# The first table of token numbers from the lists' columns by numbers in GpSimd's registers, and the last batch's ranks later

## The chip, the cores and the metric

The kernel runs on one core of one Trainium2 chip. The metric is the device time of one execution in microseconds (us). TensorE is called PE here, VectorE DVE, ScalarE ACT, GpSimd POOL and SyncE SP, as the profile calls them; PEld is PE's loading of weights. A name with a q (ACTq, SPq) is that engine's sequencer.

## The reference

Attention with rotary positions for 8 batches, 8 heads, 576 positions and a head size of 64; its output is 4608 tokens of 512 numbers. Each token then goes to one of 8 experts, the one with the largest logit, and the expert's two matrices are applied to it:

```
q_rot, k_rot = rotate(q), rotate(k)
attn = softmax(q_rot @ k_rot.T / sqrt(64));  x = attn @ v          # 4608 x 512
logits = x @ w_gate;  e_idx = argmax(logits, axis=1)               # 8 experts
gate_w = softmax(logits)[e_idx];  eom = sigmoid(x @ w_output_gate)
for e in range(8):
    mask = e_idx == e
    h = maximum(x[mask] @ w1[e], 0)                                # 512 x 1024
    out[mask] = gate_w[mask] * eom[mask, e] * (h @ w2[e])          # 1024 x 512
```

## The kernel before, in words

**Attention.** Two heads make a pair, four pairs a batch: 32 pairs, numbered 0 to 31. A pair has nine steps, so there are 288 steps g. In a step PE makes the scores of 128 query rows against 576 keys (`scores`, L468 and L461) in one of two PSUM buffers with the tag "sc"; DVE takes the row maxima (`peak`, L474); ACT makes the exponentials and frees the PSUM buffer (`exp`, L483); a step later DVE transposes them in blocks (`turn`, L489). PE's products with the values (`values`, L511) stand between the scores in four pieces per pair. POOL makes the rotated queries and keys of later pairs (`mult` L417, `add` L421, `keylo` and `querylo` L399). `Attention.step` issues the scores, the maximum and the exponential of a step, then whatever is noted for it in `todo` under four places (0 to 3), so the order on every engine is fixed by the step numbers in `EVENTS` and in the list `fs` that `place` returns.

**Ranks and lists.** After the last pair of a batch `place` works out each token's expert and its rank in that expert's list. It is spread over the following steps: `s0` (sums of the logits, L578 to L580), `s2` and `s3` (L588 on POOL, then the exponential L591 on ACT, which stands in ACT's row between two softmax steps), `s14` (ranks by two matmuls, L661 and L662, then L666 on DVE), `s17` (row and column numbers, L678 to L683), `ones` (five times: the one-hot rows `ro`, L691 on DVE, and `pl`, L693 on POOL), `s20` (the matmul L701) and `s21` (L704), which adds the batch to `lists`, a 128 x 288 table in SBUF. Column j of `lists` holds 128 places of a list; each expert owns 36 columns. For the last batch `place` returns a plain list of pieces, which the second phase takes in its order.

**The first table.** The second phase works in slots: five of 256 tokens from the batches 0 to 5 (their table is called 0), nine more of 256 and up to fifteen of 128 tokens from all of them. `table0` makes table 0 during the last attention steps, from step 266 on: PE transposes `lists` into PSUM (`turned`, L825, in a "sc" buffer), ACT copies it out and sends it to DRAM (L829 to L833), DVE works out which ten columns are wanted (`sums`, `taken`, `slots`; L762 to L799), POOL fetches those ten rows by an indirect DMA (L801), DVE decodes them (L808 to L811), PE transposes them back (L816, again a "sc" buffer) and DVE writes the numbers `0idx` (L817). At step 284 POOL gathers the tokens of the first two slots from DRAM, four indirect DMAs of 128 rows (`fetch`, `gather`, L950).

**Second phase.** For a slot PE transposes the tokens (L980), ACT and DVE split them into a high and a low half (`turn`, L995 and L996), and PE runs through eight pieces j: four products with w1 (`first`, L1015, 2.85 us each) and four with w2 (`second`, L1057, twelve matmuls each). Weights come through SP (L963) and are split by ACT (L972) and DVE (L974); in slot 0 the piece 5 is split on POOL (the condition `2 < u < 8` and `j % 4 == 1`). Results go out by indirect DMAs on POOL (L1069). After each j the method `slot` takes two pieces (one after the first two) of the list `left`: first the last batch's pieces, then those of `table1`. SP reads an expert's number into its registers by `value_load` (L961) before it loads a slot's weights.

Of the kernel before, what the change touches and what calls it, by code (L numbers as in the profile page):

```python
# [13 lines left out]
I32 = mybir.dt.int32  # L14
# [6 lines left out]
NP = H // 2  # L21
# [96 lines left out]
def body(ctx, tc, nb, offs, qk, v, rope, cst, gates, w, out):  # L118
# [115 lines left out]
class Attention:  # L234


    def __init__(self, tc, nb, pools, cc, ident, ii, first, trib, oneb, cnt, zero, qk, v, xd, row, lists):
        nc = tc.nc
        px, px2, pa2, pp1, pp2, ps_s, small, ps_a = pools
        NT = nb * S  # L240
        own = []
        self.inits = []

        def init(bd, z, rz, ac):
            nc.gpsimd.memset(ac[:, NCH - 1, :, :], 0.0)
# [12 lines left out]
        for n in range(npair):  # L258
            self.pairs.append(Pair(tc, pools, n, own[n % 2], ident, ii, rt, qk[n // NP, n % NP], v[n // NP, n % NP]))
        self.pairs[0].raw = raw0  # L260

        self.todo = {}
        self.last = []
        at = self.at
        xbs = {}

        def newxb(b):
            xbs[b] = px2.tile([P, NCH, RW], F32, tag="xb", name=f"xb{b}")

            nc.gpsimd.memset(xbs[b][QR:P, NCH - 1, DM:], 0.0)  # L270

        for n, pr in enumerate(self.pairs):
            g, b = 9 * n, n // NP
            fs = {"kh": lambda pr=pr: pr.keyhi("A"), "kl": lambda pr=pr: pr.keylo("P"),
                  "qh": lambda pr=pr: pr.queryhi("A"), "ql": lambda pr=pr: pr.querylo("P"), "lasts": pr.lasts, "den0": pr.den0, "den1": pr.den1, "den2": pr.den2, "evict": pr.evict, "back": pr.back,
                  "newxb": lambda pr=pr, b=b: newxb(b) if pr.hp == 0 else None}
            fs["divide"] = lambda pr=pr, b=b: pr.divide(xbs[b])
            for t in range(2):
                fs[f"mult{t}"] = lambda pr=pr, t=t: pr.mult("P", t)
                fs[f"add{t}"] = lambda pr=pr, t=t: pr.add("P", t)  # L280
                fs[f"load{t}"] = lambda pr=pr, t=t: pr.load(t)
                fs[f"loadv{t}"] = lambda pr=pr, t=t: pr.loadv(t)
            for k, (b0, b1) in enumerate(PIECES):
                fs[f"av{k}"] = lambda pr=pr, b0=b0, b1=b1: [pr.values(j) for j in range(b0, b1)]
            for name, o, k in EVENTS:
                if n > 1 or name not in ("load1", "load0", "mult1", "add1", "kh", "kl", "mult0", "add0", "qh", "ql")[:10 if n == 0 else 2]:
                    at(g + (3 if name == "lasts" and n == 0 else o), k, fs[name])
            if n % NP == NP - 1:
                fs = place(tc, (px, px2, small), self.pairs, b, NT, cc, trib, oneb, cnt, xbs, xd, row, lists)
                if b == nb - 1:  # L290
                    self.last = fs
                else:
                    self.nplace = 1 + max(k for k, _, _ in fs)
                    for k, p, f in fs:
                        at(g + PLACE + k, p, f)

    def done(self, b):

        return 9 * (NP * b + NP - 1) + PLACE + self.nplace

    def at(self, g, k, f):
        self.todo.setdefault((g, k), []).append(f)
# [252 lines left out]
def place(tc, pools, pairs, b, NT, cc, trib, oneb, cnt, xbs, xd, row, lists):  # L555
# [129 lines left out]
    def ones(c):  # L685

        if c == 0:
            new("ro", [P, NCH, lists.shape[1]], F32R, bufs=1)
            new("pl", [P, NCH, P], F32R, bufs=1)
            new("no", [P, NCH])  # L690
        nc.vector.tensor_scalar(T["ro"][:, c, :], row, T["hr"][:, c:c + 1], 0.0, op0=ALU.is_equal, op1=ALU.add,  # L691
                                accum_out=T["no"][:, c:c + 1])
        nc.gpsimd.tensor_scalar(T["pl"][:, c, :], row[:, 0:P], T["lo"][:, c:c + 1], T["tok"][:, c:c + 1], op0=ALU.is_equal,  # L693
                                op1=ALU.mult)

    def s20():
# [35 lines left out]
class Moe:  # L732
# [115 lines left out]
        V.tensor_tensor(out=out, in0=out, in1=num, op=ALU.min)  # L848

    def table0(self):  # L850
        V, t = self.nc.vector, self.t
        yield from self.turned(0)
        fn, fi = self.padded("fn"), t([P, E], "fi", I32)
        self.t0 = t([P, E], "t0")
        V.tensor_copy(fi, self.cnt)
        V.tensor_scalar(fi, fi, 8, None, op0=ALU.logical_shift_right)
        V.tensor_copy(fn[:, 4:], fi)
        yield
        end = self.sums(fn, "fs")
        yield  # L860
        dl = t([P, E], "fd")
        V.tensor_scalar(dl, fn[:, 4:], -2.0, float(self.rows), op0=ALU.mult, op1=ALU.add)
# [102 lines left out]
    def split(self, u):  # L965
# [215 lines left out]
```

## Time and profile before

| | |
|---|---|
| median of 3 runs | 1076.01 us (1075.89 to 1077.77) |
| the profiled execution | 1075.41 us |
| its span | 1073.6 us, mean granted PE clock 0.985 |
| attention, last softmax activation | at 556.0 us |
| PE busy | 1015.0 us, 95% of the span |
| DVE, ACT, POOL busy | 830.5, 628.0, 606.5 us |

Times inside the execution count from the span's start. A row of the timeline gives the start, the duration of the whole merged group, engine, line, operation, what is written and read, and in brackets the idle time before and what ended it. In a stretch's row "x" counts instructions; PEclk is the granted share of 2.4 GHz, so 0.50 is 1.2 GHz.

### The profile page before, as it was taken

The page shows a single profiled execution, that of the slowest core. Times are in us where ns is not written, and L with a number is a line of the kernel's source. Part 1 is how long each engine was busy: PE and PEld are TensorE (multiplying, and loading weights), DVE is VectorE, ACT ScalarE, POOL GpSimd, SP SyncE. Part 2 cuts the span into 40 slices and gives each one's busy share as a digit, 9 for nine tenths or more (in the row PEclk, how much of TensorE's full clock was granted, in tenths as well). Part 3 has the DMA queues.
Part 4 walks back from the last instruction along what each step waited for, and adds up shares of the span by engine and source line. Part 5 has one row for each costly group of instructions (what it writes and reads, how often), then busy time and mean ns, then how long its engine had stood idle before and what let it go on. Part 6 is the DMA issues. An engine that isn't in the chain of part 4 may idle for free.

```text
span 1073.6 us, 34812 instructions
## 1 busy us (share of the span) xinstructions
PE 1015.0 (95%) x14465; PEld 881.3 (82%) x14465; DVE 830.5 (77%) x1389; ACT 628.0 (58%) x1281; POOL 606.5 (56%) x594
## 2 busy tenths in 40 slices
PE   3999999999999999998989899999999999999995
PEld 3788878878788788887868788899889898899984
DVE  6888898898988888887866866657866867767772
ACT  3466665656666566665544445446765866857762
POOL 4667888788888889788332312214543533542621
PEclk9999999999999999999889999999999999999998
DMA  5556466465555666464347867766977977887860
GB/s 184 158 138 179 144 165 178 142 179 168 161 165 158 161 175 192 124 186 131 78 151 270 274 205 229 233 211 199 346 249 251 333 248 266 315 300 264 282 246 28
DMA packets 58561, 216.48 MB, mean 202 GB/s; under 512 B 9405, under 2 KB 10012, under 8 KB 54304
## 3 DMA queue, kind: packets, MB, share of 16 engines
q1 hardware_dynamic: 50304, 194.03, 57.9%
q0 software_dynamic: 6496, 18.92, 4.9%
q8 instruction: 115, 1.88, 0.7%
q10 hardware_dynamic: 1600, 1.26, 0.4%
q14 instruction: 46, 0.38, 0.1%
HBM read 196.04 MB, written 20.24 MB: 201 GB/s over the span
## 4 chain that ended last, share of the span: by engine, by line
PE 62%; DVE 12%; issue 8%; ACT 7%; POOL 6%; DMA 3%; POOLq 0%; ACTq 0%; SPq 0%; DVEq 0%
PE py L1057 17%; PE ph L1015 13%; PE sc L468 12%; PE acc L511 11%; DVE m L474 4%; PE ph L1007 4%; ACT pm L483 4%; POOL raw L417 3%; DVE pt L489 3%; PE acc L529 1%; PE mtp L980 1%; DMA v<-in_v 1%; DVE xb L536 1%; ACT wh L972 1%; ACT kh L391 1%
## 5 line engine op out<-in xcount | busy, mean ns | idle before, releaser
L483 ACT ACTIVATE pm<-sc,m 128x576 f32<-128x576 f32 x288 | 213.3, 741 | 223.4 <-DVE m L474 222.2
L974 DVE TENSOR_TENSOR wl<-wr,wh 128x1024 fp32r<-128x1024 f32 x183 | 253.4, 1397 | 48.3 <-ACT wh L972 46.8
L474 DVE TENSOR_REDUCE m<-sc 128x1 f32<-128x576 f32 x288 | 212.8, 739 | 77.8 <-PE sc L468 70.2
L468 PE MATMUL sc<-kh,q 64*128 64x288 f32 x1024 | 227.3, 329 | 29.0 <-ACT pm L483 16.3
L489 DVE STREAM_TRANSPOSE pt<-pm 128x576 f32<-128x576 f32 x288 | 219.3, 761 | 0.3 <-ACT pm L483 0.3
L1057 PE MATMUL py<-wh,ht 128*128 128x512 f32 x640 | 216.8, 403 | 0.0
L972 ACT CAST wh<-wr 128x1024 fp32r<-128x1024 f32 x208 | 212.7, 1050 | 0.4 <-ACT lt L832 0.4
L468 PEld LDWEIGHTS sc<-kh,q 64*128 64x128 f32 x1024 | 150.0, 193 | 73.3 <-ACT pm L483 39.4
L511 PE MATMUL acc<-pt,v 32*64 32x160 f32 (+1 forms) x9216 | 202.1, 299 | 4.8 <-PE sc L468 1.9
L511 PEld LDWEIGHTS acc<-pt,v 32*64 32x64 f32 x9216 | 161.3, 133 | 30.0 <-issue 23.3
L417 POOL TENSOR_TENSOR raw<-raw,rt 128x1152 f32<-128x1152 f32 x62 | 164.2, 2648 | 7.9 <-DMA raw<-in_qk 7.7
L1015 PE MATMUL ph<-xt,wh 128*128 128x256 f32 x896 | 161.8, 283 | 0.0
L1057 PEld LDWEIGHTS py<-wh,ht 128*128 128x128 f32 x640 | 121.0, 189 | 25.4
L1015 PEld LDWEIGHTS ph<-xt,wh 128*128 128x128 f32 x896 | 139.5, 190 | 1.8 <-DVE xt L996 0.4
L1015 PE MATMUL ph<-xt,wl 128*128 128x256 f32 x448 | 126.5, 282 | 0.0
L1057 PE MATMUL py<-wl,ht 128*128 128x512 f32 x320 | 126.4, 395 | 0.0
L974 POOL TENSOR_TENSOR wl<-wr,wh 128x1024 fp32r<-128x1024 f32 x25 | 61.0, 2441 | 108.5 <-ACT wh L972 102.0
L468 PE MATMUL sc<-kl,q 64*128 64x288 f32 x512 | 111.9, 300 | 0.0
L421 POOL TENSOR_TENSOR raw<-raw 128x576 f32<-128x576 f32 x62 | 88.2, 1422 | 2.4
L1031 ACT ACTIVATE ht<-ph 128x512 fp32r<-128x512 f32 x56 | 33.4, 597 | 91.1 <-PE ph L1015 91.1
L468 PEld LDWEIGHTS sc<-kl,q 64*128 64x128 f32 x512 | 85.5, 195 | 0.0
L1015 PEld LDWEIGHTS ph<-xt,wl 128*128 128x128 f32 x448 | 85.3, 190 | 0.2 <-DVE wl L974 0.2
(246 smaller groups left out, 1316.7 us busy)
## 6 DMA issues: line engine op xcount, KB each, us to landing
wr<-in_w SPq DMA_DIRECT2D x208, 512.0 KB, 5.1
raw<-in_qk SPq DMA_DIRECT2D x64, 576.0 KB, 4.0
v<-in_v SPq DMA_DIRECT2D x128, 288.0 KB, 5.0
xd<-xb SPq DMA_DIRECT2D x16, 513.0 KB, 7.3
xd<-xb SPq DMA_DIRECT2D x8, 128.2 KB, 5.0
rt<-in_rope ACTq DMA_DIRECT2D x1, 576.0 KB, 5.5
xg<-xd,2idx POOLq DMA_INDIRECT x18, 6.4
out<-y,2idx POOLq DMA_INDIRECT x18, 4.2
```

The source lines that it names most:

```text
L417: self.eng(eng).tensor_tensor(out=rv, in0=rv, in1=self.rt[:, 2 * t:2 * t + 2, x], op=ALU.mult)
L421: self.eng(eng).tensor_tensor(out=r[:, 2 * t, x], in0=r[:, 2 * t, x], in1=r[:, 2 * t + 1, x], op=ALU.add)
L468: nc.tensor.matmul(ps[:, a, :HS], self.q[r, w, c * P:c * P + P], mov[r, a * HS:a * HS + HS], start=(n == 0), stop=(n == 2))
L474: nc.vector.tensor_reduce(self.m[i], ps[:, :, :HS], axis=AX.XY, op=ALU.max, negate=True)
L483: nc.scalar.activation(pe.rearrange("p (a b) -> p a b", a=2), self.ps[i][:, :, :HS], AF.Exp, bias=self.m[i], scale=1.0, accum_out=self.z[: ...
L489: self.nc.vector.transpose(out=self.pt[:, st[0] + 5 * st[1] if st else 4, :], in_=self.pc.pop(i))
L511: nc.tensor.matmul(self.acc[h * D:h * D + D, a, o:o + 32 * n], self.v[r, h, j, :], self.pt[r, u:u + n, 32 * j:32 * j + 32], start=(j == 0) ...
L972: self.nc.scalar.copy(wh, r)
L974: eng.tensor_tensor(out=wl, in0=r, in1=wh.bitcast(F32), op=ALU.subtract)
L1007: nc.tensor.matmul(ph[:, 0, :], st[:, dc, 0:P], mv[:, dc, :], start=(n == 0), stop=(n == 11))
L1015: nc.tensor.matmul(ph[:, f, :], st[:, dc, fs], mv[:, dc, :], start=(n == 0), stop=(n == 11))
L1057: self.nc.tensor.matmul(py[h], st[:, f, hs], mv, start=(f == 0 and n == 0), stop=(f == 7 and n == 2))
```

## The change

`table0` is written anew. Six of its steps run on POOL: the number of full slots per expert (`full`, three operations on a 128 x 8 tile), their running sums (`ends`, three), the column for each slot (`passed`, three; `rows`, four), then `take`: five times a number is read into a POOL register and two columns of `lists` are copied by it, and the decoding (`flags` and `decode`, six operations on 128 x 10 tiles). DVE keeps two small reductions (`counted`), at step 259. Neither the two transposes through PSUM nor the trip through DRAM is left in table 0. Its steps are dated 255 to 269, and the gathers of the first two slots 276, where it was 284. What `table1` needs of the old table's sums (`taken`) is computed in `table1`.

For the last batch three more empty pieces stand ahead of `s14`, and `pl` (L693) is made on DVE; for other batches `V` is POOL, as before. The split of piece 5 in slot 0 goes from POOL to DVE. All later pieces of `left` come three places later.

```diff
-        g = att.done(nb - 3) + 1
-        for k, f in enumerate(pieces(moe.table0(), 19)):
-            att.at(g + k, 2 if k < 18 else 0, f)
-        att.at(g + 18, 2, moe.fetch)
+        g = att.listed(nb - 3)                       # step 262
+        for k, f in moe.table0():
+            att.at(g + k, 2, f)
+        att.at(g + 14, 2, moe.fetch)
...
-        nc.gpsimd.tensor_scalar(T["pl"][:, c, :], row[:, 0:P], ...
+        V.tensor_scalar(T["pl"][:, c, :], row[:, 0:P], ...
...
-                run(s10, s11, s12), run(s13, base), no, s14, no, s14b, run(s15, s16, s17)] + [
+                run(s10, s11, s12), run(s13, base), no, no, no, no, s14, no, s14b, run(s15, s16, s17)] + [
...
+        def full():
+            G.tensor_scalar(fn, self.cnt, 1.0 / SLOT, 0.5 / SLOT - 0.5, op0=ALU.mult, op1=ALU.add)
+            G.tensor_scalar(fn, fn, WHOLE, None, op0=ALU.add)
+            G.tensor_scalar(fn, fn, -WHOLE, None, op0=ALU.add)
+        def ends():
+            a = T["fn"]
+            for k in (1, 2, 4):
+                b = T[f"fs{k}"]
+                G.tensor_tensor(out=b[:, 4:], in0=a[:, 4:], in1=a[:, 4 - k:4 + E - k], op=ALU.add)
+                a = b
+        def passed():
+            G.tensor_scalar(T["fd"], fn, -2.0, float(self.rows), op0=ALU.mult, op1=ALU.add)
+            G.tensor_scalar(T["ge"], end, half, None, op0=ALU.is_le)
+            G.tensor_tensor(out=T["t1"], in0=T["ge"], in1=T["fd"], op=ALU.mult)
+        def counted():
+            V.tensor_reduce(T["ve"], T["ge"], axis=AX.X, op=ALU.add)
+            V.tensor_reduce(T["row"], T["t1"], axis=AX.X, op=ALU.add)
+        def rows():
+            G.tensor_tensor(out=T["row"], in0=T["row"], in1=p, op=ALU.add)
+            G.tensor_copy(ri, T["row"])
+            G.tensor_scalar(T["ve"], T["ve"], float(E - 1), None, op0=ALU.min)
+            G.tensor_copy(ei, T["ve"])
+        def take():
+            for i in range(n0):
+                r = G.value_load(ri[2 * i:2 * i + 1, 0:1], min_val=0, max_val=E * self.rows - 2)
+                G.tensor_copy(tk[:, 2 * i:2 * i + 2], self.lists[:, bass.ds(r, 2)])
...
+        return [(-7, full), (-6, ends), (-5, passed), (-3, counted), (-1, rows), (2, take), (6, flags), (7, decode)]
...
-        eng = self.nc.gpsimd if (self.todo[s][0] == 1 or 2 < u < 8) and j % 4 == 1 else self.nc.vector
+        eng = self.nc.gpsimd if self.todo[s][0] == 1 and j % 4 == 1 else self.nc.vector
```

Three places show what this moves. Line numbers of the kernel after the change differ from those before; the operands tell what is meant. The first place is POOL in pair 28; `kl` and `q` are the low halves for pair 29, `raw` after them is the rotation for pair 30. Before:

```order
L399 TENSOR_TENSOR kl_8655<-raw_8297,kh_8654 128x576
L693 TENSOR_SCALAR pl_8639<-row,lo_8539,tok_8545 128x128 x2
L399 TENSOR_TENSOR q_8729<-raw_8297,q_8729 128x576
L417 TENSOR_TENSOR raw_8609<-raw_8609,rt 128x1152
L693 TENSOR_SCALAR pl_8639<-row,lo_8539,tok_8545 128x128
L421 TENSOR_TENSOR raw_8609<-raw_8609 128x576
```

After, from the operation behind the three of `full`:

```order
L693 TENSOR_SCALAR pl_8657<-row,lo_8557,tok_8563 128x128
L874 TENSOR_TENSOR fs_118<-fn 128x8
L874 TENSOR_TENSOR fs_120<-fs_118 128x8
L874 TENSOR_TENSOR 0fs_122<-fs_120 128x8
L693 TENSOR_SCALAR pl_8657<-row,lo_8557,tok_8563 128x128
L399 TENSOR_TENSOR q_8750<-raw_8315,q_8750 128x576
L417 TENSOR_TENSOR raw_8627<-raw_8627,rt 128x1152
L878 TENSOR_SCALAR 0fd<-fn 128x8
L879 TENSOR_SCALAR 0ge<-0fs_122,ct 128x8
L880 TENSOR_TENSOR 0t_125<-0ge,0fd 128x8
L693 TENSOR_SCALAR pl_8657<-row,lo_8557,tok_8563 128x128
L421 TENSOR_TENSOR raw_8627<-raw_8627 128x576
```

Nine small operations now stand among POOL's large ones, the last three behind the product L417. On DVE two reductions of their results stand in the row of the maxima; after the change, in pair 28 (`m_7` and `m_8` are the maxima of its steps 7 and 8):

```order
L474 TENSOR_REDUCE m_7_8841<-sc_7_8834 128x1
L489 STREAM_TRANSPOSE pt_8615<-pm_6_8830 128x576
L883 TENSOR_REDUCE 0ve<-0ge 128x1
L884 TENSOR_REDUCE 0row<-0t_125 128x1
L474 TENSOR_REDUCE m_8_8890<-sc_8_8883 128x1
```

The maximum of the pair's last step is queued behind them. The second place is POOL in pairs 30 and 31, around the gathers `xg`. Before:

```order
L626 TENSOR_TENSOR ohs_9448<-ohs_9448,ohb_9388 128x8 x2
L801 DMA 0tk<-lst_84,0ri 10x128
L649 TENSOR_TENSOR base_9569<-cnt,ct 128x8
L492 TENSOR_SCALAR rz_110<-z_109 128x10
L629 TENSOR_SCALAR eg_9628<-eg_9628 128x5
L632 TENSOR_TENSOR eg_9628<-eg_9628,sm_9279 128x5
L670 TENSOR_TENSOR pr_9606<-pr_9606,oh_9310 128x40
L950 DMA xg<-xd,0idx 128x513 x4
```

After:

```order
L626 TENSOR_TENSOR ohs_9495<-ohs_9495,ohb_9437 128x8 x4
L994 DMA xg<-xd,0idx 128x513 x4
L649 TENSOR_TENSOR base_9622<-cnt,ct 128x8
L492 TENSOR_SCALAR rz_110<-z_109 128x10
L629 TENSOR_SCALAR eg_9681<-eg_9681 128x5
```

The four gathers are issued ahead of `base`, which DVE's L666 reads, and the fetch of ten rows is gone. The third place is PE in the second phase, where the last batch's ranks (`pl`) are made. Before, between two pieces of `second` of slot 0:

```order
L1057 MATMUL py_1_10347<-wl_10231,ht_0_10127 128x512
L1057 MATMUL py_1_10347<-wh_10230,ht_0_10128 128x512
L661 LDWEIGHTS oneb
L661 MATMUL pl_2_10438<-ohs_10343,oneb 128x48
L662 LDWEIGHTS trib
L662 MATMUL pl_2_10438<-ohb_10337,trib 128x40
L1057 MATMUL py_0_10346<-wh_10247,ht_0_10127 128x512
```

After, behind the first piece of `first` of slot 1:

```order
L1059 MATMUL ph_0_10498<-xt_1_10398,wh_10315 128x256
L1059 MATMUL ph_0_10498<-xt_1_10397,wl_10316 128x256
L661 LDWEIGHTS oneb
L661 MATMUL pl_2_10540<-ohs_10374,oneb 128x48
L662 LDWEIGHTS trib
L662 MATMUL pl_2_10540<-ohb_10368,trib 128x40
L1059 MATMUL ph_1_10543<-xt_1_10397,wh_10361 128x256
```

The ranks stand two pieces of PE's work later: the last of `second` and one of `first`.

## Rows read from the trace of the kernel before

**Rows 1.** Stretches: us, engines' busy time (x), PEclk, DMA share, GB/s.

```profile
428.90:445.40 16.50, 15.92 (x360) 13.45 (x359) 14.10 (x26) 10.11 (x28) 13.36 (x14) 1.00 0.54 151
494.00:517.50 23.50, 21.11 (x363) 17.47 (x362) 16.69 (x35) 10.75 (x30) 16.51 (x17) 0.78 0.27 64
428.90:474.80 45.90, 44.64 (x1044) 37.70 (x1049) 40.40 (x77) 28.53 (x75) 37.34 (x44) 1.00 0.53 148
494.00:556.00 62.00, 56.90 (x1048) 45.81 (x1052) 44.80 (x103) 28.24 (x76) 29.66 (x48) 0.83 0.40 110
506.20:516.40 10.20, 9.63 (x149) 8.20 (x150) 5.66 (x14) 3.71 (x12) 7.28 (x9) 0.50 0.11 30
543.70:553.90 10.20, 10.18 (x132) 6.71 (x121) 3.03 (x7) 1.68 (x5) 4.91 (x8) 0.50 0.44 131
594.90:598.30 3.40, 3.40 (x10) 2.61 (x9) 3.30 (x9) 0.46 (x1) 0.00 (x0) 0.50 0.80 235
```

**Rows 2.** Timeline of PE, around the old table's two transposes.

```profile
506.77 0.85 PE L468 MATMUL sc<-kh,q 64*128 64x288 f32 x2 [1.77 <-ACT pm L483]
...
542.88 0.22 PE L816 MATMUL 0tr<-ident,0tk 10*128 10x10 f32 x1 [1.23 <-ACT pm L483]
543.04 6.36 PE L511 MATMUL acc<-pt,v 32*64 32x160 f32 x80
...
551.72 2.39 PE L511 MATMUL acc<-pt,v 32*64 32x160 f32 x64
```

**Rows 3.** Timeline of POOL in pair 28.

```profile
484.19 1.57 POOL L693 TENSOR_SCALAR pl<-row,lo,tok 128x128 fp32r<-128x128 bf16 x2
486.32 1.42 POOL L399 TENSOR_TENSOR q<-raw,q 128x576 fp32r<-128x576 f32 x1 [0.57 <-ACT q L391]
487.68 2.66 POOL L417 TENSOR_TENSOR raw<-raw,rt 128x1152 f32<-128x1152 f32 x1
```

**Rows 4.** Groups on POOL, 60 to 500 us: busy us, mean ns, idle before.

```profile
L399 POOL TENSOR_TENSOR q<-raw,q 128x576 fp32r<-128x576 f32 x27 | 38.3, 1420 | 25.1 <-ACT q L391 25.1
L399 POOL TENSOR_TENSOR kl<-raw,kh 128x576 fp32r<-128x576 f32 x27 | 38.1, 1409 | 28.4 <-ACT kh L391 28.4
...
L679 POOL TENSOR_SCALAR hr<-hr 128x5 f32<-128x5 f32 x6 | 1.4, 236 | 0.5
```

**Rows 5.** Timeline of DVE in pair 28, the maximum of its last step.

```profile
490.86 0.76 DVE L474 TENSOR_REDUCE m<-sc 128x1 f32<-128x576 f32 x1 [0.54 <-PE sc L468]
```

**Rows 6.** Timeline of POOL, then of ACT, in pair 25.

```profile
441.79 0.27 POOL L588 TENSOR_TENSOR dd<-lgs,mx 128x40 f32<-128x40 f32 x1
...
442.30 0.23 ACT L591 ACTIVATE ex<-dd 128x40 f32<-128x40 f32 x1
```

**Rows 7.** Line 961, SP's register loads: least, median, most ns.

```profile
L961 SPq TENSOR_LOAD <-1ei x12: 268/273/1017, 706.3 to 1020.3; - x12
```

**Rows 8.** Timeline of POOL: first and last of the four gathers.

```profile
543.60 1.12 POOL L950 DMA_INDIRECT xg<-xd,0idx  x1 [3.47 <-DVE 0idx L817]
...
547.66 1.00 POOL L950 DMA_INDIRECT xg<-xd,0idx  x1 [0.30 <-issue]
```

**Rows 9.** Waits of PE, 500 to 660 us: total us, times, longest.

```profile
PE pl L661 <- DVE ohs L626: 2.8, 1, 2.8
PE pl L701 <- POOL pl L693: 2.1, 2, 1.7
```

**Rows 10.** Timeline of PE at the last batch's ranks.

```profile
594.41 0.20 PE L661 MATMUL pl<-ohs,oneb 128*128 128x48 bf16 x1 [2.75 <-DVE ohs L626]
...
598.89 0.40 PE L1015 MATMUL ph<-xt,wh 128*128 128x256 f32 x2
```

**Rows 11.** Timeline of DVE in slot 0.

```profile
581.09 2.86 DVE L974 TENSOR_TENSOR wl<-wr,wh 128x1024 fp32r<-128x1024 f32 x1 [0.49 <-ACT wh L972]
...
595.41 0.68 DVE L996 TENSOR_TENSOR xt<-mtp,xt 128x512 fp32r<-128x512 f32 x1
```

**Rows 12.** The page, part 5: the splits L974 on DVE.

```profile
L974 DVE TENSOR_TENSOR wl<-wr,wh 128x1024 fp32r<-128x1024 f32 x183 | 253.4, 1397 | 48.3 <-ACT wh L972 46.8
```

More of the change, by code (lines that the diff above doesn't have):

```diff
@@ L53 @@
 PLACE, PM = 20, 3
+LISTED = 35
 TURN = 1
@@ L292, in __init__, with listed @@
                 else:
-                    self.nplace = 1 + max(k for k, _, _ in fs)
                     for k, p, f in fs:
                         at(g + PLACE + k, p, f)
-    def done(self, b):
-        return 9 * (NP * b + NP - 1) + PLACE + self.nplace
+    def listed(self, b):
+        return 9 * (NP * b + NP - 1) + PLACE + LISTED
     def at(self, g, k, f):
@@ L692, in ones @@
                                 accum_out=T["no"][:, c:c + 1])
-        nc.gpsimd.tensor_scalar(T["pl"][:, c, :], row[:, 0:P], T["lo"][:, c:c + 1], T["tok"][:, c:c + 1], op0=ALU.is_equal,
+        V.tensor_scalar(T["pl"][:, c, :], row[:, 0:P], T["lo"][:, c:c + 1], T["tok"][:, c:c + 1], op0=ALU.is_equal,
                                 op1=ALU.mult)
@@ L721, in place @@
           (12, 2, adds(1, 2)), (13, 2, adds(3, 4)), (15, 2, s8), (15, 2, base), (17, 1, s14), (17, 2, s14b), (18, 2, s9),
-          (19, 2, lambda: (s10(), s11())), (20, 2, s15), (22, 2, lambda: (s16(), s12())), (23, 2, s17), (35, 1, s20), (35, 2, s21)]
+          (19, 2, lambda: (s10(), s11())), (20, 2, s15), (22, 2, lambda: (s16(), s12())), (23, 2, s17), (LISTED, 1, s20), (LISTED, 2, s21)]
     fs += [(26 + c, 3, lambda c=c: ones(c)) for c in range(NCH)]
@@ L850, in table0 @@
     def table0(self):
[L851 to L862, printed above, removed]
@@ L863, in table0 @@
-        self.taken(self.t0, fn[:, 4:], end, self.n0)
-        yield
-        yield from self.slots(0, 2 * self.n0, end, dl, None, 2, 5, 2)
+        V, G, t = self.nc.vector, self.nc.gpsimd, self.t
+        m, n0 = 2 * self.n0, self.n0
+        sl = self.cc(C_SL)
+        half, p = sl[:, 0:1], sl[:, 1:2]
+        T = {"fn": self.padded("fn"), "fs1": self.padded("fs1"), "fs2": self.padded("fs2")}
+        for n, sh in (("fs4", [P, 4 + E]), ("fd", [P, E]), ("ge", [P, E]), ("t1", [P, E]), ("row", [P, 1]), ("ve", [P, 1])):
+            T[n] = t(sh, f"0{n}")
@@ new lines, in table0 @@
+        fn, end = T["fn"][:, 4:], T["fs4"][:, 4:]
+        self.f0 = fn, end
+        ei, ri = t([P, 1], "0ei", I32), t([P, 1], "0ri", I32)
+        self.ei[0] = ei, 2
+        tk, g1, g2 = (t([P, m], f"0{n}") for n in ("tk", "g1", "g2"))
+        idx = self.idx[0] = t([P, m], "0idx", I32)
+        def full():
+            G.tensor_scalar(fn, self.cnt, 1.0 / SLOT, 0.5 / SLOT - 0.5, op0=ALU.mult, op1=ALU.add)
+            G.tensor_scalar(fn, fn, WHOLE, None, op0=ALU.add)
+            G.tensor_scalar(fn, fn, -WHOLE, None, op0=ALU.add)
@@ new lines, in flags, with decode @@
+        def flags():
+            G.tensor_scalar(g1, tk, 0.0, BIG, op0=ALU.is_equal, op1=ALU.mult)
+            G.tensor_scalar(g2, tk, 0.0, -1.0, op0=ALU.is_gt, op1=ALU.mult)
+            G.tensor_tensor(out=g1, in0=g1, in1=g2, op=ALU.add)
+        def decode():
+            G.tensor_scalar(tk, tk, -number(self.NT, 0), None, op0=ALU.add)
+            G.tensor_tensor(out=tk, in0=tk, in1=g1, op=ALU.add)
+            G.tensor_copy(idx, tk)
+        return [(-7, full), (-6, ends), (-5, passed), (-3, counted), (-1, rows), (2, take), (6, flags), (7, decode)]
@@ L885, in table1 @@
         if self.n0:
+            self.t0 = t([P, E], "t0")
+            self.taken(self.t0, *self.f0, self.n0)
             V.tensor_tensor(out=pn[:, 4:], in0=pn[:, 4:], in1=self.t0, op=ALU.subtract)
```

## The prediction

> **What bounds the kernel now.** I read the page first: PE is nearly always busy, so only stretches where PE waits or runs slowly can give time. Then the stretches, cut at the first softmax activation of a pair: the attention repeats every four pairs, so pairs 29, 30 and 31 (494.0 to the ninth activation of pair 31 at 556.0) must compare with pairs 25, 26 and 27 (428.9 to 474.8). The reader is to see 62.00 against 45.90 us for the same softmax steps, with a granted clock of 0.83 against 1.00 [rows 1]. So the last three pairs lose 16.1 us. Next the timeline of PE in them: two waits for ACT, 1.77 us before 506.77 and 1.23 us before 542.88, each at a transpose of table 0 through a score buffer or just behind it, and right after each a stretch of 10.2 us at 0.50, the lower level of 1.2 GHz [rows 1, 2]. Pair 29 alone takes 23.50 us where pair 25 took 16.50. The same view in the second phase shows a wait for the last batch's one-hot rows (2.75 us, then 3.4 us at 0.50) and one for POOL's `pl` (2.1 us) [rows 1, 9, 10]. Last the timelines of POOL and DVE in pairs 25 and 28, to see who would be late with more work on POOL.
>
> **The change part by part.** All sums are against the profiled execution, 1075.41 us (span 1073.6 and 1.8 around it); the median of the runs is 0.6 higher, which I add at the end.
>
> *Table 0 off PE, ACT and DVE: -16.1 us.* The two transposes, the copies and DMA issues on ACT and some twenty small DVE operations go. With them go the causes of both waits of PE, and so the half-speed stretches behind them. I take the whole excess of 16.1 us. What could stay of it is the slow piece at 543.04: 80 records of the values' product in 6.36 us. At the same low clock 64 take 2.39 us, so 80 would take 3.0; 3.4 us of it the clock does not explain [rows 2]. It lies exactly beside the four gathers, 543.60 to 548.66 [rows 8]; that is the first rival.
>
> *Small work on POOL: +2.5 us.* Full, ends, passed and rows are 13 operations. A small operation took 0.24 us [rows 4]; with the gap behind a dependent one I count 0.3, so 3.9 us. Two places feel it.
> First `counted` on DVE in pair 28. POOL starts two `pl` at 484.19; with full and ends before and between them they end at 484.19 + 1.57 + 1.8 = 487.6, `q` at 489.0 (its 0.57 us wait is used up), the product at 491.6, passed at 492.5 [rows 3]. DVE would be free for `counted` at 490.86 - 0.54 = 490.3 [rows 5]. So it waits 2.2 us, and the maximum behind it starts some 2.0 us late, with ACT's exponential and PE's next scores but one waiting on it. DVE idled 0.54 us just there, and such gaps take up part of it: I take 1.2 of between 0 and 2.0.
> Second `dd` on POOL in pair 29, which ACT's `ex` reads: in pair 25 it ended at 442.06 and `ex` started at 442.30, a margin of 0.24 us [rows 6]. Ahead of it stand 3.9 us of small operations and five register loads with a copy each. Such a load is not on POOL in this trace; on SP it took 0.27 us in the median and 1.02 at most [rows 7], so with a copy of 0.24 five take 2.6 to 6.3 us. POOL's own waits take up 0.57 us in pair 28 [rows 3], 0.93 and 1.05 in pair 29 (25.1 and 28.4 us over 27 pairs [rows 4]) and the 1.2 by which everything is late already: 6.5 - 3.75 leaves 2.7 us late, less whatever of the loads runs beside `kl` (the sequencer loads, the engine computes). I take 1.0 us of between 0 and 6, and 0.3 for DVE's reciprocal, which waits for POOL a pair later.
> The Trainium skill speaks against putting loads there: its page "DMA: Bandwidth & Descriptors", section "Latency and other measured facts", gives a floor of about 600 ns for a `tensor_load`. The median on SP is under half of that [rows 7], so the measurement decides; by the page five loads would add 1.7 us and the sum would end at 1059.0.
>
> *Gathers eight steps earlier: 0.* They now stand ahead of `base`, which DVE needs at step 280. In pair 30 POOL has no rotations left (they are for pairs that do not exist), so I expect it at the gathers before the last pair starts, and the four, 5.1 us [rows 8], end about when `base` is needed.
>
> *Ranks of the last batch later: -3.3 us.* PE waited from 591.66 to 594.41, and its twelve matmuls of the last w2 piece then ran to 598.89, 1.7 us of that for half the speed over 3.4 us [rows 1, 10]. Without the ranks there the twelve end at 591.66 + 2.8 = 594.5. Next late is DVE: slot 1's first product needs the second half of its tokens, which DVE finished at 596.09 [rows 11], since DVE itself was behind, not PE. DVE gets POOL's split of piece 5, 1.40 us [rows 12], and loses the collision with it (a split of 2.86 us [rows 11]); the two about cancel, 0.5 us in DVE's favour. So PE starts at 595.6, where it was 598.89. Bounds: no wait at all -4.4; DVE no earlier and the clock falling again -1.1.
>
> *`pl` on DVE: -1.8 us.* PE's waits of 2.1 us for POOL [rows 9] go. DVE gets five operations of 128 columns. One on POOL took 0.79 us [rows 3]; a DVE operation of 1024 columns took 1.40 [rows 12], an eighth of which is 0.17. I take 0.3, so 1.5 us over slot 1, of which PE may see 0.3. Bounds: -2.1 to 0.
>
> Sum: -16.1 + 2.5 - 3.3 - 1.8 = -18.7, so 1056.7 in place of 1075.41, and 1057.3 as a median. The terms' bounds give 1052 to 1063.
>
> **The rivals.**
> *The slow piece belongs to the gathers (0.25).* For: both start within 0.1 us and the row of products behind the gathers has its usual pace for that clock. Against: it also starts with the fall of the clock, and the gathers could not show in the second phase, where matmuls are longer. Then 3.4 us go to pair 31's start, where PE again has a piece of values' products, and the gathers of slot 2, no longer behind POOL's split, meet those of the last pair, about 2 us; with a little lower clock 1064.
> *POOL's loads are slow (0.12).* If a load holds POOL for 1.0 us or more, `dd` is 6 us late, ACT waits, PE idles over 1.77 us and the clock falls as at 506: the fall and its wait cost pair 29 7.0 us [rows 1]. 1057.3 + 6 + 5 = 1068.
> *DVE takes over both waits of the second phase (0.08).* Ranks and `pl` then give nothing: 1057.3 + 5.1 = 1062.
> *Slower than before (0.05).* The one mechanism that reaches so far is the second one with a larger price: lateness of `dd` passes to ACT one to one, and about 5 us come with the low clock. To eat 18.7 us the loads must be some 14 us late, so about 3.3 us each, over three times the longest on SP; at 4 us each 1079.
>
> **How the numbers follow.** The forecast holds with 0.50, with its own range 1053 to 1061. The others as said. The range 1052 to 1069 leaves out the slower case, the upper part of the slow loads, and a few hundredths below. Within 0.2% (2.2 us, about what a measurement of this kernel can tell from no change) of the time before is only a narrow strip between slow loads and the slower case: 0.02. Faster: 0.50 + 0.25 + 0.08 and nearly all of 0.12, so 0.92. Slower 0.06.
>
> **What the profile after would show.** Pair 29 at 17 to 18 us and the three pairs at 48 to 50, with the granted clock at 1.00 throughout; a wait of DVE's `0ve` for POOL of about 2 us at 490; ACT's `ex` waiting 1 us for `dd`; POOL's five loads within 3 us. In the second phase no wait of PE at L661 or L701, but one under 1.5 us at the first product of slot 1 for DVE's `xt`. Wrong would be: a stretch at 0.50 in pairs 28 to 31, products of the values at 0.08 us a record beside the gathers, or PE waiting for POOL's `q` or `kl` in pair 30 or 31.

## The result and the profile after

The changed kernel takes 1066.09 us (median of 9 executions, 1063.62 to 1071.14); the kernel before took 1076.01 in the same comparison (9 executions). The ratio is 0.9912, with a 95% interval of 0.9889 to 0.9935: 9.5 us faster by the ratio and 9.9 by the medians, where 18.7 were forecast. The time lies in the stated range, but it is not the forecast's: it is close to the 1064 of the first rival. The profiled execution took 1066.09 us (span 1064.2, mean granted clock 0.992).

Stretches of the kernel after, columns as in [rows 1]: pairs 28, 29, 30 and 31 (this one to its ninth activation), then pairs 29 to 31 together, two stretches at half speed, the last products of the values (ninth activation to slot 0's first product), slot 0 and slot 1.

```profile
476.80:494.60 17.80, 15.84 (x351) 13.13 (x349) 15.95 (x36) 10.06 (x27) 17.04 (x23) 1.00 0.70 198
494.60:511.70 17.10, 16.52 (x361) 13.89 (x360) 13.93 (x26) 10.11 (x28) 14.81 (x23) 1.00 0.31 75
511.70:531.30 19.60, 16.14 (x352) 13.30 (x352) 13.85 (x27) 10.10 (x27) 15.68 (x30) 0.99 0.40 96
531.30:550.10 18.80, 16.73 (x314) 14.08 (x322) 12.55 (x26) 7.42 (x21) 1.96 (x9) 0.77 0.61 184
494.60:550.10 55.50, 49.40 (x1026) 41.26 (x1032) 40.33 (x77) 27.63 (x74) 32.44 (x61) 0.92 0.45 119
531.00:534.10 3.10, 2.80 (x12) 2.71 (x12) 2.18 (x4) 2.37 (x8) 0.00 (x0) 0.50 1.04 273
544.30:551.10 6.80, 6.80 (x141) 5.76 (x137) 4.52 (x9) 2.49 (x6) 1.40 (x7) 0.51 0.02 5
550.10:565.28 15.18, 11.44 (x351) 8.85 (x339) 9.43 (x23) 5.91 (x11) 8.71 (x9) 0.96 0.58 148
565.28:591.41 26.13, 26.13 (x170) 23.40 (x168) 18.66 (x40) 14.96 (x23) 0.00 (x0) 1.00 0.73 272
591.41:617.85 26.44, 25.40 (x163) 22.21 (x162) 22.91 (x52) 12.39 (x17) 4.12 (x4) 1.00 0.92 292
```

The last three of these stretches in the kernel before:

```profile
556.00:567.40 11.40, 8.64 (x329) 7.38 (x316) 9.36 (x23) 5.78 (x11) 4.30 (x7) 1.00 0.44 123
567.40:598.89 31.49, 28.21 (x170) 24.57 (x170) 22.72 (x49) 15.51 (x23) 6.50 (x3) 0.95 0.79 281
598.89:626.11 27.22, 25.15 (x161) 22.24 (x160) 17.46 (x38) 12.03 (x18) 11.35 (x9) 1.00 0.79 250
```

Pairs 29 to 31 fell from 62.00 us [rows 1] to 55.50, where 48 to 50 were forecast; with pair 28 the last softmax activation comes 5.9 us earlier (550.1 for 556.0). Then 3.8 us are given back: the last products of the values take 15.18 us for 11.40. Slot 0 gains 5.4, slot 1 0.8, all later slots 1.1. Together that is the 9.4 us between the two spans (1073.6 and 1064.2). Two stretches at 0.50 stand in pair 31, which the prediction named as a sign that it is wrong.

The waits of PE from 500 to 660 us in the kernel after (total, times, longest), to be held against [rows 9]:

```profile
PE acc L511 <- issue: 3.8, 5, 1.6
PE acc L661 <- ACT ac L520: 3.1, 1, 3.1
...
PE ph L1059 <- DVE xt L1040: 0.5, 1, 0.5
PE pl L701 <- DVE xt L1040: 0.5, 1, 0.5
```

The waits for `ohs` and `pl` are gone as forecast. A wait of 3.1 us is new, and it stands where pair 31 begins. The timelines around it, of POOL, PE, ACT, DVE and SP:

```profile
524.51 1.29 POOL L994 DMA_INDIRECT xg<-xd,0idx  x1 [0.67 <-issue]
...
528.72 0.99 POOL L994 DMA_INDIRECT xg<-xd,0idx  x1 [0.30 <-issue]
...
524.66 1.89 PE L511 MATMUL acc<-pt,v 32*64 32x160 f32 x64
...
527.77 0.43 PE L468 MATMUL sc<-kh,q 64*128 64x288 f32 x2
531.30 0.22 PE L661 MATMUL acc<-ohs,oneb 128*128 128x48 bf16 x1 [3.10 <-ACT ac L520]
...
530.34 0.58 ACT L518 COPY ac<-acc 128x512 f32<-128x512 f32 x1 [3.88 <-remote]
...
530.42 0.76 DVE L474 TENSOR_REDUCE m<-sc 128x1 f32<-128x576 f32 x1 [4.12 <-remote]
...
530.33 1.71 SPq L412 DMA_DIRECT2D v<-in_v  x4
```

PE's products end at 526.55 and its scores at 528.2 by their rows, but ACT's eviction of these products, DVE's maximum of these scores and SP's loads into the buffer of values all start within 0.1 us of 530.35. All three wait for PE alone, and PE's three updates of its semaphore stand in the trace at 530.32, 530.39 and 530.47. So PE's signals came up to 3.8 us behind the ends of their rows. (The profile models the ends of PE's rows, so the products themselves may have ended late; for what waits on them that is the same.) They came when the four gathers (524.51 to 529.71) had ended. "Remote" is the profile's word for a release that it couldn't assign.

### The profile page after: what moved, and what is told of

Its sections match the earlier page's. It is cut to its first block, busy times and chain, and to the rows that moved or that the text cites. A ratio compares the mean times of both kernels' runs of the same rounds, so it can differ in the third digit from the quotient of the medians.

```text
span 1064.2 us, 34833 instructions
## 1 busy us (share of the span) xinstructions
PE 1007.4 (95%) x14461; PEld 875.6 (82%) x14461; DVE 827.4 (78%) x1377; ACT 627.3 (59%) x1279; POOL 600.3 (56%) x610
## 4 chain that ended last, share of the span: by engine, by line
PE 61%; DVE 14%; POOL 8%; issue 7%; ACT 6%; DMA 3%; another core or an unknown queue 0%; ACTq 0%; POOLq 0%; DVEq 0%
PE py L1101 17%; PE ph L1059 14%; PE sc L468 11%; PE acc L511 10%; DVE m L474 4%; PE ph L1051 4%; ACT pm L483 4%; POOL raw L417 4%; DVE pt L489 2%; DVE wl L1018 2%; DMA v<-in_v 2%; PE mtp L1024 1%; PE acc L529 1%; POOL q L399 1%; POOL raw L421 1%
## 5 line engine op out<-in xcount | busy, mean ns | idle before, releaser
L511 PE MATMUL acc<-pt,v 32*64 32x160 f32 (+1 forms) x9216 | 198.5, 297 | 7.7 <-issue 3.8
L417 POOL TENSOR_TENSOR raw<-raw,rt 128x1152 f32<-128x1152 f32 x62 | 164.1, 2646 | 7.7 <-DMA raw<-in_qk 7.4
L1018 POOL TENSOR_TENSOR wl<-wr,wh 128x1024 fp32r<-128x1024 f32 x24 | 58.3, 2430 | 90.0 <-ACT wh L1016 84.9
```

Of the source, the lines that this page charges most:

```text
L417: self.eng(eng).tensor_tensor(out=rv, in0=rv, in1=self.rt[:, 2 * t:2 * t + 2, x], op=ALU.mult)
L511: nc.tensor.matmul(self.acc[h * D:h * D + D, a, o:o + 32 * n], self.v[r, h, j, :], self.pt[r, u:u + n, 32 * j:32 * j + 32], start=(j == 0) ...
```

## The experiments

All are edits of the changed kernel. A ratio is to the kernel before on the same chip.

**Gathers at step 284, as before**

```diff
-        att.at(g + 14, 2, moe.fetch)
+        att.at(g + 22, 2, moe.fetch)
```

> The changed kernel with the gathers of the first two slots back at step 284, eight steps later. Theory A (the gathers themselves hold up PE, wherever they stand): pair 30 takes 15.8 us in place of 19.6, no completion of PE comes 3.8 us late at its end, and pair 31 has instead a slow or late stretch of 3 us beside the gathers; in all about the time of the changed kernel, 1064 to 1068. Theory B (the traffic of weights and values holds up PE): the 3.1 us wait of PE ahead of the ranks of pair 31 stays where it is, 1066. In both the wait of PE for its code near 541 us (1.9 us) may go, since PE gets to it later.

Measured: 1064.39 us (4 executions), ratio 0.9901 (0.9870 to 0.9933). Pair 30 takes 16.2 us and pair 31 19.3; the gathers run from 535.89 to 541.09, and PE's products of the values beside them take 5.6 us (536.88 to 542.51) where 1.6 is usual:

```profile
536.88 1.62 PE L511 MATMUL acc<-pt,v 32*64 32x160 f32 x50
538.73 0.26 PE L511 MATMUL acc<-pt,v 32*64 32x128 f32 x1 [0.22 <-issue]
539.80 2.71 PE L511 MATMUL acc<-pt,v 32*64 32x128 f32 x29 [0.81 <-issue]
```

The wait of 3.1 us ahead of pair 31's ranks is gone: the hold-up moved with the gathers, theory A. Not all of the 5.6 us is theirs: the 0.81 us is a stop that PE makes at this place in every kernel (last section), and from 540.17 the clock is at 0.50.

**Gathers at step 270**

```diff
-        att.at(g + 14, 2, moe.fetch)
+        att.at(g + 8, 2, moe.fetch)
```

> The changed kernel with the gathers of the first two slots at step 270, right behind the numbers they need, six steps earlier, where no other transfer runs. Theory A: the hold-up moves with them: PE loses 2 to 4 us early in pair 30, none at its end; 1064 to 1068. Theory B: the wait at the end of pair 30 stays, 1066. Theory A2 (gathers hold up PE only beside other transfers): no hold-up at all, pair 30 takes 16 to 17 us, 1061.

Measured: 1069.35 us (10 executions), ratio 0.9943 (0.9917 to 0.9969). Pair 30 takes 24.5 us, at a granted clock of 0.79. PE beside the gathers (516.74 to 521.94), then POOL and DVE:

```profile
518.77 1.27 PE L511 MATMUL acc<-pt,v 32*64 32x160 f32 x49
520.28 0.51 PE L511 MATMUL acc<-pt,v 32*64 32x160 f32 x5 [0.23 <-issue]
521.01 0.45 PE L511 MATMUL acc<-pt,v 32*64 32x128 f32 x5 [0.22 <-issue]
521.73 0.51 PE L511 MATMUL acc<-pt,v 32*64 32x160 f32 x5 [0.28 <-issue]
522.48 0.91 PE L511 MATMUL acc<-pt,v 32*64 32x160 f32 x16 [0.24 <-issue]
525.61 0.84 PE L468 MATMUL sc<-kh,q 64*128 64x288 f32 x2 [2.21 <-ACT pm L483]
...
523.49 0.26 POOL L492 TENSOR_SCALAR rz<-z 128x10 f32<-128x10 f32 x1
...
523.79 0.22 DVE L495 RECIPROCAL rz<-rz 128x10 f32<-128x10 f32 x1 [6.30 <-POOL rz L492]
523.92 0.70 DVE L474 TENSOR_REDUCE m<-sc 128x1 f32<-128x576 f32 x1
```

Forty-nine products run at the usual pace, then five at a time with gaps: 4.6 us (518.77 to 523.39) where 1.6 is usual. No weights or values were loaded beside them, so theory A2 falls and A holds for the products. But the 8 us that pair 30 loses are not the price of this hold-up. In this kernel POOL's `rz` stands behind the four gathers, DVE's reciprocal waits 6.3 us for it, and the maximum behind the reciprocal starts at 523.92 only, though its scores have been ready since 517.5. That is the softmax for which PE waits 2.2 us, and from 522.35 the clock is at 0.50 for 10.2 us. The time lies above all three theories.

**Plain loads in the gathers' place**

```diff
-        self.gather(0)
-        self.gather(1)
+        for k in range(4):
+            self.nc.scalar.dma_start(out=xg[:, k, :], in_=self.xd[k * P:k * P + P, :])
```

> The changed kernel with the four gathers of the first two slots replaced at the same place by four plain loads of 128 fixed rows each on ACT's queue; the tokens of these two slots are therefore fixed rows, not the chosen ones. Theory A1 (it is GpSimd's issuing of an indirect DMA that holds up PE): pair 30 takes 15.8 to 16.5 us, no late completion, 1059 to 1062. Theory A3 (it is the arrival of rows in SBUF): the late completion stays, 1066.

Measured: 1061.17 us (4 executions), ratio 0.9868 (0.9837 to 0.9899). Pair 30, 0.55 of its span with transfers, at 16.20 us; then pair 31 and PE in it:

```profile
513.10:529.30 16.20, 15.92 (x357) 13.52 (x357) 13.83 (x27) 9.97 (x26) 11.29 (x26) 1.00 0.55 142
529.30:546.50 17.20, 14.99 (x335) 12.60 (x338) 12.48 (x26) 7.46 (x21) 1.96 (x9) 0.90 0.63 177
```

```profile
539.64 0.79 PE L511 MATMUL acc<-pt,v 32*64 32x128 f32 x29 [1.95 <-issue]
```

The same bytes into the same buffer do not hold up PE: theory A3 falls. (These loads read neighbouring rows, the gathers scattered ones; the two differ in that as well as in the queue.) In pair 31 PE stops for 1.95 us all the same, and the clock is at 0.50 from 540.69 to 544.10. So this half-speed stretch of pair 31 does not need the gathers.

**The third slot's gathers later**

```diff
+            if j == 6 and s:
+                self.gather(s + 2)
             if j == 7:
                 self.store(s)
-            if j == 6:
-                self.gather(s + 2)
+                if s == 0:
+                    self.gather(2)
```

> The changed kernel with the gathers of the third slot issued behind the stores of the first, so about 35 us later. Theory A: PE's gaps of 1.35 and 0.7 us in the last products of the values (560.7 to 562.8 us) go, the second phase starts about 2 us earlier, 1064. Theory B: the gaps stay, since the weights' loads run there all the same, 1066.

Measured: 1068.03 us (7 executions), ratio 0.9921 (0.9892 to 0.9950): no gain. In the profile the last products of the values take 11.56 us in place of 15.18, 190 of them without a gap, so the third slot's gathers do cost 3.6 us there. But the second half of slot 1 takes 18.6 us for 14.1, since the tokens for slot 2, the third slot, are now asked for only at 597.2. The gain was given back, and neither theory's time (1064, 1066) came out.

**The two reductions of the table later**

```diff
-        return [... (-3, counted), (-1, rows), ...]
+        return [... (-1, counted), (0, rows), ...]
```

> The changed kernel with the two reductions on DVE two steps later (step 261) and POOL's rows one step later (262). Theory C (DVE's wait of 1.9 us for POOL makes PE wait 1.0 us at 493.8, and PE's clock then falls in part of the executions): no wait of PE at the end of pair 28, which takes 16.9 us in place of 17.8; pair 29 at a granted clock of 1.00 in every execution, 16.5 to 17.3 us; median 1062.5 to 1064.5, since 0.9 us goes always and 1 to 3 us of a slow stretch in part of the runs. Theory D (the slow stretches in pair 29 come from POOL's five register reads): pair 29 still varies between 17 and 20 us, 1065.

Measured: 1065.62 us (6 executions, 1059.26 to 1068.11), ratio 0.9899 (0.9869 to 0.9930). Pair 28 takes 16.9 us, as theory C says, but pair 29 17.5. The wait of ACT in this kernel:

```profile
ACT ex L591 <- POOL dd L588: 2.3, 1, 2.3
```

This view of the waits gave 0.8 in the changed kernel. The softmax is earlier, POOL is not, and what was won in pair 28 is waited for in pair 29. The median does not tell this kernel from the changed one; it is theory D's time, with theory C's pair 28.

**Gathers at step 280**

```diff
-        att.at(g + 14, 2, moe.fetch)
+        att.at(g + 18, 3, moe.fetch)
```

> The changed kernel with the gathers of the first two slots behind base and the sums for pair 30's reciprocal, at step 280: they start when pair 30's last exponential is done, about 526.5, and run while PE makes scores, ranks and the pair's transposes, with few products of the values beside them. Theory A4 (only the dense rows of products with the values are held up): pair 30 takes about 16 us and pair 31 loses under 1.5 us, 1061 to 1063. Theory A (any work of PE is held up, its signals too): 2 to 4 us are lost in the first steps of pair 31, 1064 to 1067.

Measured: 1058.39 us (4 executions, 1057.99 to 1059.64), ratio 0.9842 (0.9813 to 0.9870). The gathers now stand behind POOL's sum for pair 30's reciprocal, which waits for the last exponential. The timeline of POOL, a row of PE, then the stretches of pairs 30 and 31 and of the last products:

```profile
527.11 0.25 POOL L492 TENSOR_SCALAR rz<-z 128x10 f32<-128x10 f32 x1 [2.54 <-ACT pm L483]
527.97 1.29 POOL L994 DMA_INDIRECT xg<-xd,0idx  x1 [0.60 <-issue]
```

```profile
538.56 0.79 PE L511 MATMUL acc<-pt,v 32*64 32x128 f32 x29 [0.38 <-issue]
```

```profile
512.30:528.50 16.20, 15.94 (x357) 13.53 (x357) 13.81 (x27) 9.94 (x26) 11.82 (x27) 1.00 0.33 75
528.50:544.10 15.60, 14.52 (x322) 11.58 (x325) 12.39 (x26) 7.46 (x21) 5.75 (x13) 1.00 0.83 264
544.10:557.50 13.40, 11.13 (x345) 8.40 (x326) 9.41 (x23) 5.82 (x11) 8.63 (x9) 1.00 0.51 150
```

Beside the gathers PE makes scores, ranks and transposes, and loses nothing; only the first products of the values, from 531.73 on and so beside the last two, take 3.25 us for 1.6. No clock falls in these pairs. Four steps of one edit are worth 7.7 us, by the medians. Theory A4 holds for the hold-up, but the time is under its range of 1061 to 1063. The kernels without any hold-up (plain loads 1061.17, gathers that move no rows 1062.49) are slower too: in them PE stops for 1.95 us in pair 31 and half speed follows, while here the same stop takes 0.38 us and none follows. That part of the gain no theory had foreseen.

**A pause between the weights' loads**

```diff
-        moe.begin0()
+        for u in range(4):
+            if u == 2:
+                nc.sync.dma_start(out=lst[0][0:1, 0:1], in_=att.pairs[-1].m[5][0:1, :])
+            moe.load(u)
```

> The changed kernel in which the third and fourth weight loads of slot 0 wait on SP for a small store of a maximum of pair 31's sixth step (four bytes to an unused row in DRAM), so that the transfer engines are free from about 537 to 541 us. Theory E (PE runs out of code at 540.8 because the fetch of its next 256 instructions comes 5 us late behind the weights' loads): no gap of 1.9 us there, the fetch starts at 536 to 538; pair 31 is 1.5 to 5 us shorter if no other fetch comes late; 1061 to 1064. Rival F (the gap is an aftermath of the gathers): it stays, 1066.

Measured: 1061.87 us (4 executions, 1060.29 to 1069.06), ratio 0.9887 (0.9848 to 0.9926). The fetch of code starts at 539.94 instead of 540.30, not at 536 to 538: theory E is not borne out in its main point. PE's gap is 1.1 us instead of 1.9 (by its weight loads; by its products 0.8 and 1.6), and no half-speed stretch follows it; pair 31 takes 16.4 us instead of 18.8. The pause did not bring the fetch forward, so it did not test the theory. Rival F falls by the plain loads above, where the gap is there without any gathers. What delays the fetch stays open.

**The table alone**

```diff
-                ... no, no, no, no, s14, no, s14b, ...
+                ... no, s14, no, s14b, ...
...
-        V.tensor_scalar(T["pl"][:, c, :], row[:, 0:P], ...
+        nc.gpsimd.tensor_scalar(T["pl"][:, c, :], row[:, 0:P], ...
...
-        eng = self.nc.gpsimd if self.todo[s][0] == 1 and j % 4 == 1 else self.nc.vector
+        eng = self.nc.gpsimd if (self.todo[s][0] == 1 or 2 < u < 8) and j % 4 == 1 else self.nc.vector
```

> The changed kernel with the second phase as before: last batch's ranks not delayed, its pl on POOL, the split of piece 5 of slot 0 on POOL. By the prediction's terms (3.3 and 1.8) it is 5.1 us slower than the changed kernel, 1071. If the gathers of the third slot, which POOL's split again holds back, cost 2 to 3.6 us in the changed kernel, it is only 1.5 to 3 us slower, 1068 to 1069.

Measured: 1069.28 us (6 executions), ratio 0.9933 (0.9910 to 0.9955): 3.2 us over the changed kernel by the medians, with intervals that overlap. In the profile, which is of the slowest of the six executions (1072.19), slots 0 and 1 take 60.0 us against 52.6, the last products 12.8 against 15.2: the edits of the second phase give 7.4 there and take 2.4 ahead of it.

**Reads later, with the gathers at step 280**

```diff
-        att.at(g + 14, 2, moe.fetch)
+        att.at(g + 18, 3, moe.fetch)
...
-        return [... (-3, counted), (-1, rows), (2, take), (6, flags), (7, decode)]
+        return [... (-1, counted), (0, rows), (6, take), (9, flags), (10, decode)]
```

> As the kernel with the gathers at step 280, and the two reductions on DVE at step 261, the rows at 262, and POOL's five register reads at step 268, behind dd (flags 271, decode 272). Theory G (POOL's work on the table delays the softmax in two places, and what is taken away at the first is waited for at the second): with both gone pair 28 takes 16.9 us (17.8 before), pair 29 16.5 to 17.0 at a granted clock of 1.00 (18.6 before), no wait of ACT's ex for dd over 0.3 us; 1054.5 to 1056.5 against 1058.4. Rival H (the waits only move on, to POOL's low halves of pair 30's keys): pair 30 becomes 1.5 to 3 us longer, 1058.

Measured: 1061.07 us (5 executions, 1058.40 to 1063.50), ratio 0.9865 (0.9843 to 0.9887). Pairs 28 and 29 take 16.90 and 16.40 us at a clock of 1.00, pair 30 17.40 where step 280 alone has 16.20: a part of the gain goes as rival H says. The rest is lost in the last products, 15.27 us at 0.89 for 13.40, beside the third slot's gathers (548.83 to 553.45). The median is above both theories and above step 280 alone, though the intervals overlap.

**The split back on GpSimd, with the gathers at step 280**

```diff
-        att.at(g + 14, 2, moe.fetch)
+        att.at(g + 18, 3, moe.fetch)
...
-        eng = self.nc.gpsimd if self.todo[s][0] == 1 and j % 4 == 1 else self.nc.vector
+        eng = self.nc.gpsimd if (self.todo[s][0] == 1 or 2 < u < 8) and j % 4 == 1 else self.nc.vector
```

> As the kernel with the gathers at step 280, and the split of piece 5 of slot 0 back on POOL, which then holds back the third slot's gathers to about 575. Theory A (these gathers slow the last products of the values, 550 to 555 us): from the last softmax activation to slot 0's first product 11.4 to 12 us in place of 13.4; DVE is then relieved of 1.4 us too; 1056.5 to 1057. Rival I (DVE's split collides with POOL's, and slot 1's tokens come later): slot 0 is 1 to 2 us longer, 1058 to 1059.

Measured: 1057.35 us (4 executions), ratio 0.9834 (0.9811 to 0.9857). The last products, slot 0 and slot 1:

```profile
544.14:555.14 11.00, 8.62 (x330) 7.36 (x318) 8.96 (x22) 5.81 (x11) 4.31 (x7) 1.00 0.40 114
555.14:581.38 26.24, 26.24 (x169) 23.50 (x168) 18.66 (x43) 13.89 (x21) 6.47 (x3) 1.00 0.81 300
581.38:608.90 27.52, 25.40 (x163) 22.20 (x162) 23.98 (x53) 13.45 (x18) 4.23 (x4) 1.00 0.93 292
```

The third slot's gathers now stand behind POOL's split (570.11), and the last products take 2.4 us less than the 13.40 at step 280. Slot 0 stays as it was, slot 1 takes 1.0 longer (27.52 for 26.50).

**All three**

The edits of the last two kernels in one.

> Gathers at step 280, reductions and register reads later as in the first of this call, and the split back on POOL as in the second. If the parts add up: 1052.5 to 1055.5, which is 20 to 23 us under the kernel before. If the softmax's waits come back elsewhere, 1056 to 1058.

Measured: 1055.74 us (5 executions, 1054.73 to 1057.43), ratio 0.9811 (0.9794 to 0.9827), 20.8 us under the kernel before. This is the fastest version by the median, and its interval lies clear of the changed kernel's, but not of those of step 280 alone (0.9813 to 0.9870) and of the split back (0.9811 to 0.9857). What the later reads add is thus not shown.

**Gathers that move no rows**

```diff
-        self.gather(0)
-        self.gather(1)
+        self.gather(0, 0)
+        self.gather(1, 0)
...
-    def gather(self, s):
+    def gather(self, s, top=None):
...
-                ... bounds_check=n - 1, oob_is_err=False)
+                ... bounds_check=n - 1 if top is None else top, oob_is_err=False)
```

> The changed kernel with its four gathers of the first two slots at the same place (step 276), but with an upper bound of 0 for the row numbers, so that nearly every row is out of bounds and is not moved; the tokens of these two slots are zeros, which are set at the start. Theory J (POOL's making of an indirect DMA holds up PE, whether or not rows move): PE's completions at the end of pair 30 come 3 to 4 us late all the same, pair 30 takes 19 to 20 us, 1066 to 1068. Theory K (it is the rows' small transfers on the queue that POOL feeds): no late completion, pair 30 takes 16.2 us, 1060 to 1062 as with plain loads.

Measured: 1062.49 us (4 executions), ratio 0.9893 (0.9833 to 0.9953); the kernel before spread from 1062.91 to 1079.39 on this chip, so only the profile decides. POOL, then the products beside its four gathers:

```profile
526.35 1.29 POOL L996 DMA_INDIRECT xg<-xd,0idx  x1 [0.19 <-issue]
...
530.56 1.00 POOL L996 DMA_INDIRECT xg<-xd,0idx  x1 [0.30 <-issue]
...
526.98 1.38 PE L513 MATMUL acc<-pt,v 32*64 32x160 f32 x64
...
540.58 1.36 PE L513 MATMUL acc<-pt,v 32*64 32x128 f32 x29 [1.95 <-issue]
```

POOL spends the same 5.2 us, PE runs at its usual pace (64 in 1.38 us) and pair 30 takes 16.2 us. Theory J falls: the hold-up needs rows that are moved through POOL's queue; POOL's 5.2 us on the four transfers do not make it alone. The stop of 1.95 us in pair 31, the last row, is there without it, with half speed from 540.63 to 550.88.

## Why the prediction was half right

**The failed step** is "Gathers eight steps earlier: 0." It asked only whether POOL has time for them and when `base` is due; both came out (four gathers by 529.7, DVE's ranks at 534.5). It did not carry over what its own first rival said: that the slow piece beside the gathers in [rows 2] belongs to them. With that, a place beside products of the values costs PE. At step 276 it cost pair 30 3.4 us: the five profiled kernels with the gathers there take 19.5 to 20.9 us for it, five others (step 280, step 284, plain loads, no rows, the split back) 16.2 to 16.3. The first half-speed stretch of pair 31 follows the wait of 3.1 us. The second does not come from the gathers, since plain loads and gathers without rows have it too; it follows PE's stop of 1.95 us there (1.6 in the changed kernel), for which the prediction had no term. 1058.39 at step 280 is close to the forecast's 1057.3, but that is in part luck: this stop happened to shrink to 0.4 us, the last products still lose 2.0 us (13.40 for 11.40), and the second phase gives 1.1 more than forecast.

**The range.** The measured time lies in it because it was set by the rivals. The bounds of the terms do not give the 1063 that the prediction says: with 8.3 for POOL (2.0, 6 and 0.3), -1.1 and 0 they end at 1067.

**The rival's chance.** Its "against" was weak: that the slow piece also starts with the fall of the clock. Its "for" was misread: the piece starts at 543.04 and the gathers at 543.60, so 0.56 us apart, not 0.1. The other plain reading of [rows 2], that 3.4 us were not explained by the clock, was the better one. The rival had the kind and the sum right (1064), but the place wrong: pair 30's end, not pair 31's start. Its second part, the third slot's gathers beside the last products, was priced at 2 us and cost 2.4 to 3.6.

**Table 0 gone, -16.1.** Nearly right, once the gathers are out of the way: at step 280 pairs 30 and 31 take 31.8 us against 38.5 (62.00 less 23.50 in [rows 1]), and pair 29 takes 16.4 once POOL's reads stand later. Three pairs took 49.1 us at best (the split back, with pair 29 at 17.1), within the 48 to 50 forecast; some 3 us over pairs 25 to 27 stay.

**Small work on POOL, +2.5.** The waits came as worked out, and smaller. DVE, ACT, and POOL's third read in the kernel after, then the reads on POOL's sequencer (least, median, most ns):

```profile
491.72 0.16 DVE L883 TENSOR_REDUCE 0ve<-0ge 128x1 f32<-128x8 f32 x1 [1.72 <-POOL 0ge L879]
...
509.47 0.24 ACT L591 ACTIVATE ex<-dd 128x40 f32<-128x40 f32 x1 [0.78 <-POOL dd L588]
...
503.67 0.18 POOL L895 COPY 0tk<-lists 128x2 f32 x1 [0.52 <-issue]
```

```profile
L894 POOLq TENSOR_LOAD <-0ri x5: 288/291/494, 501.3 to 504.4; - x5
```

DVE waited 1.7 us (forecast 2.2), ACT 0.8 (1.0). A read took 0.29 in the median, near the 0.27 on SP in [rows 7], so that was the right guide and the rivals of slow reads fall. A read with its copy recurred every 0.70 us (0.52 and 0.18 in the row), where 0.51 was counted; five take 3.5. The Trainium skill's floor of about 600 ns for a `tensor_load` ("DMA: Bandwidth & Descriptors", "Latency and other measured facts") does not show here either. Pairs 28 and 29 lost 0.9 and 0.6 us in this execution. Not forecast: PE's wait of 1.0 us that follows DVE's at 493.8 stood in nine of the profiled executions, and in six of them the clock fell to 0.50 right behind it, and pair 29 took 18.3 to 19.8 us; in three it did not, and pair 29 took 17.1. It may be one reason why the changed kernel's times spread over 7.5 us; only one of its executions was profiled.

**Ranks later, -3.3, and pl on DVE, -1.8.** Slot 0 gained 5.4 and slot 1 0.8, 6.2 together for 5.1. DVE was less late than thought: PE waits 0.5 us for `xt` and slot 0 runs without a gap. But the edit that moved the split also freed the third slot's gathers, and the stretch ahead of slot 0 lost 3.8.

## What to carry to other kernels

Before a gather is moved, look at what PE does beside it: here it was free beside scores, transposes and the wide products of the second phase (slot 0 of the split back: PE busy 26.24 of 26.24 us, with gathers at 570.11), and cost 2.4 to 3.6 us beside dense products of 32 rows. Look also at what stands behind it on its own queue: at step 270 the costliest wait was that of DVE for POOL's `rz`, behind the gathers. When an operation leaves a queue, look at what it held back; the third slot's gathers ran ahead as soon as the split was gone. A lateness removed at one consumer of a busy engine is waited for at the next until the engine's own work is moved.

## What the runs showed of the hardware

Rows gathered through POOL's queue hold up PE's dense products of 32 rows and its signals, the signals by up to 3.8 us, while the same bytes through ACT's queue and gathers without rows do not. By what path, and whether the queue or the scattered rows matter, stays open. Missing code is not the reason: in the step-280 kernel the products have gaps of up to 0.3 us between 532.8 and 533.9, though the packet of code before had landed at 525.90, the next was started at 536.08, and PE's rows run on between the two.

PE also stops at one fixed place of its code in pair 31, behind its 21,697th record (products and weight loads counted together). In the changed kernel:

```profile
542.71 0.79 PE L511 MATMUL acc<-pt,v 32*64 32x128 f32 x29 [1.62 <-issue]
```

It does so in every profiled execution after the change, idle for 0.4 to 2.2 us. Each time it goes on 1.2 to 1.5 us after a packet of 16 KB on an instruction queue has landed (here landed at 541.38, on at 542.71). That this queue is PE's is worked out: it moves 115 such packets, and PE alone has as many as 29,028 records. In five kernels the stop was 0.8 us or less with no gathers beside it, and no half speed followed; in seven it was 1.4 us or more, and the clock fell to 0.50 at it or within 2 us behind it in six of them. In the kernel before, this place lay within the slow piece and could not be seen.
